# Column maxima of the pooling logits through DRAM, W_out's squares summed over all blocks before one norm product, and a new order

## The chip, the cores and the metric

The kernel runs on one core of one Trainium2 chip. The core has five engines that run side by side, each through its own list of instructions in order: TensorE (PE in the profile, with its weight loads as PEld), VectorE (DVE), ScalarE (ACT), GpSimd (POOL) and SyncE (SP), which here issues nearly all DMA transfers. An instruction waits on semaphores for what it needs from other engines or from a transfer, and everything behind it on its engine waits too. The metric is the device time of one execution in microseconds, the median over runs; lower is better.

## The reference, cut to what matters

```python
a = exp(phi - max(phi, over the 576 positions)); a = a / (sum(a) + 1e-9)
k_m = einsum('bhsm,bhsd->bhmd', a, k)       # 8 batches, 8 heads, 576 positions,
v_m = einsum('bhsm,bhsd->bhmd', a, v)       # 64 dims, pooled to 32 memory rows
scores = q @ k_m.T / 8
attn = exp(scores - max(scores)); attn = attn / (sum(attn) + 1e-9)
x = attn @ v_m                              # 4608 tokens x 512
h = x @ w_in                                # 512 x 2048
g = h - tanh(h)
out = g @ w_out                             # 2048 x 512
```

The weights arrive as 64-bit floats and are converted on the chip. Every float is carried as a sum of two fp16 parts, high and low (`hi`, `lo` for weights, `ah`, `al` for the attention, `ph`, `pl` for v_m times w_in), and a product is three fp16 matmuls. For `g` a short polynomial in h is used that holds for small h. A check of the sizes of the data decides at the end whether that was allowed; if not, a slow path (`wide_path`) recomputes everything. For that check the kernel sums the squares of W_in's and W_out's columns.

## The kernel before, in words

The order of the work is one table, `ORDER`: each word is a step with its indices, and the kernel records the steps in that order. `in_order` then ties every instruction to the one before it on its engine, so the table fixes each engine's list. A step with several parts (a Python generator) appears as often as it has parts: `H0.0 ... H0.0` is the matmuls first and the square later. An `x` behind a word chooses the other PSUM buffer.

The words that matter here:

- `i6:kv3`, `o2:gg`, `k1:q`: a load of a weight block of W_in, of W_out, or of a block for the check, into the buffer named behind the colon. `T` converts a pair of blocks (lines 447, 450, 453 on VectorE, then 464 on ScalarE), and `L`, `Lv`, `Lp` make the low part on GpSimd, VectorE or TensorE.
- `FX`, `FQ`, `FA`: loads of the pooling logits of a batch, once as rows (`pt`, for the maximum) and once turned (`e`, for the products). `KA`, `KB`, `KR`, `Q`, `QT`: loads of k and v, and of q; `QT` uses the buffer `qt`.
- `X`, `XP`, `Y` or `YM`, `YE`: the softmax of the logits (below). `V`: pooling on TensorE (line 271). `N`: its norm on VectorE. `U`, `UV`: the transposition and its high and low parts.
- `S`, `AM`, `AE`, `AD`, `AT`, `AS`: scores, softmax and its two fp16 halves (`ah`, line 562; `al`, line 564), in two halves of the positions. A `v` marks VectorE in place of GpSimd.
- `P`, `PL`: v_m times w_in and its low part. The tokens come in 18 units of 256 and the 2048 columns of W_in in four blocks: `H` (line 622, 24 matmuls of 256 columns) makes h for one unit and block, `a` or `ap` the cubic on VectorE and ScalarE (lines 642, 644, 646), `g`, `c`, `f`, `s` the fp16 parts, `M` (lines 750 and 769) the product with W_out, `E` and `O` the output.
- `CW`, `SI`, `SS`, `NI`, `SO`, `NO`: the check's window of the weights (lines 495 and 496 on ScalarE or 498 on VectorE) and the sums of squares of W_in and W_out. `Z`: matmuls on constants, which keep TensorE busy while the first data come.

In batches 0 and 1 the softmax of the logits runs on rows. In batches 2 to 7, `X` (`top`) takes each row's maximum over the positions (line 191), giving a value per partition for two halves, and multiplies the identity by it (line 193, `dg`, in the buffer `qt`). `XP` (`top_all`) multiplies ones by `dg` on TensorE (line 202, fp32), so that every partition holds all 256 maxima in PSUM (`pmx`). `Y` subtracts them from `e` on VectorE, straight from PSUM (lines 210 and 213, batches 2 and 3). `YM` has ScalarE copy them to SBUF (line 221, `ms`) and GpSimd subtract (batches 4 to 7). `YE` is the exponential.

For W_out's norms, `SO` squares a quarter of the matrix (line 521), `SS` adds its four blocks of 128 rows to one (line 508), and `NO` multiplies by ones, four matmuls for four blocks of columns (line 529), with a copy to `wn` (line 531). Four quarters make 16 matmuls, and VectorE adds the four results (line 535).

Of the kernel before, what the change touches and what calls it, by code (L numbers as in the profile page):

```python
# [71 lines left out]
Z0.0 i0:gg i1:gg T0 T0 T0 T0 Z0.0 Z0.0 Z0.0 Z0.0 Z0.0 i6:kv3 T3 T3 T3 Z0.0 Z0.0 Z0.0 Z0.0 Z0.0 FX0 T3 Z0.0 Z0.0 Z0.0 Z0.0 Z0.0 X0 Lp0 Lp0 YX0 Z0.0  # L72
Z0.0 Lp3 Lp3 Z0.0 XT0 i2:gg i3:pp5 T1 T1 T1 i4:kv2 T1 XT0 XU0x T2 KA0 XU0 Z0.0 T2 T2 V0.0 Z0.0 Z0.0 Lv1 KB0 V0.1 N0 T2 L2 L2 U0x UV0 o2:gg Z0.0 Z0.0
o3:gg Z0.0 T9 T9 T9 U0 Q0.0 S0.0x S0.0 Q0.1 S0.1 UV0 KA1 P0.0x P0.0 P0.1 PLp0.0 AM0.0 AM0.0 AE0.0 P0.1 PLp0.1 o4:gg o5:pp2 S0.1 AM0.1 AM0.1 AD0.0
AD0.0 AE0.1 AD0.1 W0 AT0.0 T10 T9 AD0.1 AT0.1 PLp0.1 AS0.0 Q1.0 AS0.0 PLp0.0 Lp9 H0.0x ASv0.1 T10 ASv0.1 H1.0 Lp9 T10 T10 L10 o6:gg o7:gg H1.1 H0.0
# [4 lines left out]
g2.0 M2.0 i12:kv2 T12 T12 T12 Y2 a2.1 CW1 H3.0 c2.0 T12 a2.1 Lv4 o11:gg T13 T13 P0.2 P0.2 M2.0 a2.1 H3.1 i14:kv3 g2.1 KA2 c2.1 ap3.0 FA3 PL0.2 YE2  # L80
Lv12 ap3.0 ap3.0 V2.0 V2.1 T6 P1.2x T13 M2.1 H3.1 M2.1 T6 T6 T13 g3.0 a3.1 N2 U2x P1.2 Lv13 PL1.2 a3.1 OP2 T6 OP2 UV2 T7 T7 T7 H0.2x H0.2 a3.1 g3.1 T7
Lv6 H1.2 H1.2 M3.0 c3.0 M3.0 a0.2 Lv7 ap1.2 a0.2 a0.2 P0.3 o12:kv2 T14 ap1.2 o14:kv3 Q2.1 BS0 U2 c3.1 g0.2 M3.1 M3.1 c0.2 P0.3 PL0.3 H1.3x ap1.2 T15
OP3 OP3 UV2 H0.3 T15 g1.2 H1.3 FQ3 c1.2 T15 H0.3 M0.2 T15 L15 a1.3 a1.3 S2.1 T14 T14 T14 S2.0x a0.3 a0.3 S2.1 S2.0 P1.3x P1.3 a1.3 g1.3 a0.3 P2.0 g0.3
AMv2.0 PL1.3 M0.2 L14 c1.3 c0.3 H2.2 H2.2 AMv2.0 AM2.1 AM2.1 a2.2 AE2.0 ADv2.0 P2.0 a2.2 H2.3 H2.3 a2.3 M1.2 M1.2 PL2.0 a2.2 BF0 g2.2 cv2.2 H3.2 L15
P2.1 H3.2 L14 M1.3 a2.3 a2.3 BH0 BL0 M1.3 ADv2.0 W2 AT2.0 ap3.2 P2.1 R1 O1 O1 AE2.1 ap3.2 ap3.2 PL2.1 BS1 BF1 AS2.0 AS2.0 M0.3 M0.3 H4.0 H4.0 ap4.0 R0
P2.2 H3.3 g2.3 c2.3 O0 O0 BH1 BL1 AD2.1 AD2.1 ap4.0 ap4.0 M2.2 R2 X3 g3.2 c3.2 P2.2 PL2.2 H3.3 H4.1 H4.1 ap3.3 ap3.3 g4.0 ap4.1 ap4.1 KR3.0 XP3 Y3
f4.0 s4.0 M2.2 QT3.0 ap3.3 g3.3 s4.0 YE3 cv4.0 M2.3 M2.3 H4.2 O2 O2 c3.3 ap4.1 AT2.1 R3 H4.2 BS2 P2.3 AS2.1 P2.3 g4.1 AS2.1 V3.0x PL2.3 ap4.2 ap4.2
BF2 BH2 M3.2 f4.1 ap4.2 f4.2 M3.2 H4.3x s4.1 KR3.1 s4.1 BL2 V3.1 N3 k4:q XX M3.3 M3.3 H4.3 ap4.3 ap4.3 g4.2 U3x U3 UV3 M4.0 M4.0 cv4.1 UV3 S3.0x ap4.3
O3 O3 P3.0 M4.0 M4.0 S3.0 AMv3.0 P3.0 M4.1 H5.0 BS3 AMv3.0 AE3.0 f4.3 k0:e g4.3 cv4.3 M4.1 M4.1 M4.1 PL3.0 c4.2 s4.2 s4.2 P3.1 H5.0 a5.0 a5.0 M4.2
sv4.3 H5.1 CW4 BF3 a5.0 BH3 BL3 H5.1 g5.0 k2:q c5.0 M4.2 M4.2 f5.0 QT3.1 M4.2 H5.2 s5.0 sv4.3 M4.3 P3.1 a5.1 ADv3.0 a5.1 M4.3 M4.3 PL3.1 S3.1 ADv3.0  # L90
s5.0 a5.1 AT3.0 M4.3 H5.2 S3.1 E4 g5.1 a5.2 a5.2 E4 CW2 f5.1 E4 E4 sv5.1 P3.2 M4.3 H5.3 H5.3 FQ4 M5.0 FA4 M5.0 a5.2 cv5.1 E4 E4 AS3.0 a5.3 sv5.1 M5.0
M5.0 CW0 AS3.0 H6.0 M5.1 M5.1 M5.1 M5.1 f5.2 a5.3 g5.2 KR4.0 cv5.2 s5.2 s5.2 a5.3 H6.0 a6.0 f5.3 a6.0 a6.0 P3.2 H6.1 s5.3 H6.1 f6.0 M5.2 M5.2 M5.2
M5.2 P3.3 g5.3 c5.3 s5.3 M5.3 ap6.1 ap6.1 PL3.2 H6.2 ap6.1 g6.1 P3.3 AM3.1 AM3.1 c6.1 AE3.1 X4 XP4 g6.0 M5.3 c6.0 s6.0 PL3.3 f6.1 H6.2 a6.2 KR4.1 M5.3
Ev5 Ev5 M5.3 s6.0 Ev5 Ev5 Ev5 a6.2 ADv3.1 ADv3.1 YM4 M5.3 s6.1 Ev5 a6.2 YM4 YE4 H6.3 H6.3 s6.1 QT4.0 AT3.1 ap6.3 ap6.3 M6.0 M6.0 AS3.1 AS3.1 g6.2 k3:e
f6.2 M6.0 sv6.2 V4.0 M6.1 M6.1 ap6.3 g6.3 f6.3 M6.0 M6.1 M6.1 sv6.3 sv6.2 H7.0 H7.0 a7.0 c6.2 V4.1 N4 W3 a7.0 sv6.3 M6.2 SI0 H7.1 a7.0 f7.0 H7.1 a7.1
U4 UV4 FQ5 UV4 M6.2 QT4.1 M6.2 a7.1 M6.2 U4 H7.2 H7.2 SSv0 NI0 a7.1 f7.1 a7.2 c6.3 M6.3 NI0 g7.0 a7.2 a7.2 s7.0 S4.0 c7.0 S4.0 AMv4.0 M6.3 M6.3 E6
s7.0 g7.2 c7.2 H7.3 H7.3 E6 a7.3 M6.3 E6 s7.1 E6 E6 W4 g7.1 M6.3 E6 s7.1 P4.0 P4.0 S4.1x S4.1 AMv4.1 a7.3 X5 CW3 AMv4.0 AE4.0 a7.3 g7.3 M7.0 M7.0 M7.0
M7.0 H8.0 H8.0 f7.2 c7.1 M7.1 M7.1 M7.1 M7.1 s7.2 f7.3 PL4.0 ap8.0 ap8.0 AMv4.1 AD4.0 ap8.0 XP5 s7.2 k5:e sv7.3 CW5 cv7.3 M7.2 KR5.0 AD4.0 f8.0 g8.0
M7.2 M7.2 M7.2 sv7.3 AE4.1 ADv4.1 s8.0 s8.0 c8.0 AT4.0 H8.1 YM5 ADv4.1 H8.1 P4.1 P4.1 M7.3 M7.3 a8.1 a8.1 a8.1 H8.2 AS4.0 PL4.1 M7.3 Ev7 H8.2 a8.2 FA5
QT5.0 YM5 a8.2 YE5 f8.1 M7.3 Ev7 P4.2 P4.2 g8.1 M7.3 AS4.0 c8.1 s8.1 s8.1 Ev7 Ev7 a8.2 g8.2 Ev7 H8.3 M8.0 Ev7 M8.0 c8.2 M8.0 V5.0 M8.1 AT4.1 AS4.1  # L100
KR5.1 PL4.2 H9.0 H8.3 a8.3 a8.3 a8.3 H9.0 f8.2 a9.0 a9.0 s8.2 s8.2 M8.1 M8.1 V5.1 f8.3 P4.3x P4.3 N5 s8.3 k6:e M8.0 M8.1 g8.3 H9.1x H9.1 a9.0 PL4.3
U5x s8.3 UV5 ap9.1 f9.0 M8.2 M8.2 UV5 ap9.1 ap9.1 c8.3 f9.1 M8.2 M8.2 M8.3 g9.0 c9.0 M8.3 SI1 k7:q SS1 U5 S5.0 g9.1 M8.3 sv9.0 k8:e E8 E8 H9.2 E8 E8
S5.0 M8.3 M8.3 AS4.1 H9.2 H9.3x sv9.0 CW6 ap9.2 ap9.2 ap9.2 QT5.1 c9.1 M9.0 M9.0 M9.0 E8 E8 s9.1 s9.1 AM5.0 H9.3 a9.3 AM5.0 f9.2 a9.3 FQ6 a9.3 NI1x
# [33 lines left out]
class Attention:  # L137


    def __init__(self, tc, c, big, place, ins):  # L140
# [47 lines left out]
    def top(self, b, d):  # L188
        nc, big = self.tc.nc, self.big
        mx = big.tile([P, 2], F32, tag="mx", name=f"mx{b}")  # L190
        nc.vector.tensor_reduce(mx, d["pt"], axis=AX.X, op=ALU.max)
# [1 line left out]
        nc.vector.tensor_tensor(
            dg, self.c["ident"].unsqueeze(1).to_broadcast((P, 2, P)),
            mx.unsqueeze(2).to_broadcast((P, 2, P)), op=ALU.mult,
# [945 lines left out]
```

## Time and profile before

| | |
|---|---|
| median of 3 runs | 635.82 us (635.75 to 637.44) |
| the profiled execution | 636.29 us |
| its span, first to last instruction | 634.2 us |
| granted TensorE clock, mean | 0.996 |
| TensorE busy | 619.4 us |
| VectorE busy | 570.9 us |
| ScalarE, GpSimd busy | 428.7, 350.5 us |
| moved by DMA | 85.03 MB |

In the profile, a group's row gives line, engine, operation, output from input by the names in the kernel, shape and count, then busy time in all and the mean of one in ns, then the idle time ahead of it and who ended it. A row of waits gives who waited for whom, the total in us, how often, and the longest. A row of the timeline gives start and duration in us. The rows by stretch give busy time and count of instructions for each engine, the granted clock (1 is full), the share of the DMA engines' time and GB/s. Durations of neighbouring matmuls overlap, so what one holds the array for is read from start to start.

### The profile page before, as it was taken

The numbers are of one execution on the slowest core, as the hardware profiler recorded it, in microseconds if no ns is written. First come the engines' busy times: TensorE is split into PE (matmuls) and PEld (weight loads), VectorE is DVE, ScalarE is ACT, GpSimd is POOL, SyncE is SP. The second block draws the span as 40 slices with busy tenths as digits, with TensorE's granted clock in tenths as the row PEclk, the third lists the DMA queues.
The fourth block names the chain that finished last, engine by engine and source line by source line (L and its number), as shares of the span: only waits on it lengthen the run. The fifth ranks groups of instructions, "written<-read, shape, count | busy, mean of one in ns | idle before, by whom it ended". The sixth has DMA issues, their size and how long they took to land.

```text
span 634.2 us, 16291 instructions
## 1 busy us (share of the span) xinstructions
PE 619.4 (98%) x6908; PEld 485.5 (77%) x6908; DVE 570.9 (90%) x763; ACT 428.7 (68%) x601; POOL 350.5 (55%) x314
## 2 busy tenths in 40 slices
...
GB/s 342 416 269 274 252 264 158 118 73 68 184 138 145 65 56 72 73 167 112 116 85 122 113 67 149 109 88 173 38 41 163 118 103 89 49 153 35 166 100 39
DMA packets 25872, 85.03 MB, mean 134 GB/s; under 512 B 2752, under 2 KB 2752, under 8 KB 25024
## 3 DMA queue, kind: packets, MB, share of 16 engines
...
## 4 chain that ended last, share of the span: by engine, by line
PE 86%; DVE 7%; DMA 4%; ACT 1%; issue 1%; SPq 0%; DVEq 0%; ACTq 0%
PE h L622 27%; PE x L769 22%; PE o L769 16%; PE o L750 10%; PE pp L573 3%; PE o1h L750 3%; DMA raw<-in_w_out_dram 3%; PE pkv L271 2%; DMA pt<-in_phx_dram 1%; PE psc L323 1%; DVE h L642 1%; DVE wt L450 1%; DVE wt L453 1%; DVE h L646 1%; DVE bw L709 0%
## 5 line engine op out<-in xcount | busy, mean ns | idle before, releaser
L622 PE MATMUL h<-ah,ph 128*128 128x256 f16 (+3 forms) x1536 | 201.0, 246 | 0.7 <-DVE h L642 0.7
L622 PEld LDWEIGHTS <-ph 128*128 128x128 f16 x2304 | 178.2, 98 | 20.7 <-issue 3.7
L672 POOL TENSOR_TENSOR g<-h,g 128x512 f16<-128x512 f32 x114 | 128.3, 1147 | 100.4 <-ACT g L666 94.2
L622 PE MATMUL h<-al,ph 128*128 128x256 f16 (+3 forms) x768 | 170.0, 246 | 1.1 <-POOL al L564 1.1
L693 POOL TENSOR_TENSOR f<-s,f 128x512 f16<-128x512 f32 x86 | 107.3, 1269 | 86.1 <-ACT f L689 81.1
L769 PEld LDWEIGHTS <-f 128*128 128x128 f16 x1344 | 129.1, 98 | 20.8 <-issue 5.2
L769 PE MATMUL x<-bt,f 128*128 128x256 f16 x1008 | 128.3, 273 | 0.0
L644 ACT ACTIVATE u<-u,beta 128x1024 f32<-128x1024 f32 x72 | 82.5, 1146 | 46.8 <-DVE h L642 46.5
L769 PEld LDWEIGHTS <-g 128*128 128x128 f16 x1008 | 97.9, 98 | 14.7 <-issue 3.5
L629 ACT ACTIVATE u<-h 128x1024 f32<-128x1024 f32 x72 | 73.3, 1018 | 47.6 <-PE h L622 31.4
L642 DVE SCALAR_TENSOR_TENSOR h<-h,u 128x1024 f32<-128x1024 f32 x72 | 87.9, 1221 | 19.2 <-ACT u L629 17.6
L646 DVE SCALAR_TENSOR_TENSOR h<-u,h 128x1024 f32<-128x1024 f32 x72 | 92.7, 1289 | 11.7 <-ACT u L644 11.4
L666 ACT ACTIVATE g<-h 128x512 f16<-128x512 f32 (+2 forms) x128 | 68.2, 579 | 19.9 <-DVE h L646 13.4
L750 PEld LDWEIGHTS <-g 128*128 128x128 f16 x384 | 36.7, 98 | 45.2 <-issue 3.0
L689 ACT ACTIVATE f<-s 128x1024 f16<-128x1024 f32 x56 | 58.6, 1048 | 11.1 <-DVE s L682 7.0
L750 PE MATMUL o<-wout_hi,g 128*128 128x512 f16 x192 | 59.0, 379 | 0.0
L680 DVE TENSOR_TENSOR s<-h 128x512 f32<-128x512 f32 x56 | 45.3, 808 | 2.0 <-DVE h L646 0.5
L769 PE MATMUL o<-wout_hi,f 128*128 128x256 f16 x224 | 45.9, 273 | 0.0
L769 PE MATMUL o<-wout_hi,g 128*128 128x256 f16 x224 | 45.8, 273 | 0.0
L769 PE MATMUL x<-wout_hi,g 128*128 128x256 f16 x224 | 45.8, 273 | 0.0
L769 PE MATMUL o<-bt,g 128*128 128x256 f16 x336 | 45.3, 273 | 0.0
L586 ACT ACTIVATE ph<-pp 128x1024 f16<-128x1024 f32 x32 | 32.4, 1014 | 18.4 <-PE pp L573 17.6
...
## 6 DMA issues: line engine op xcount, KB each, us to landing
...
chk<-in_w_in_dram SPq DMA_DIRECT2D x16, 512.0 KB, 4.1
chk<-in_w_out_dram SPq DMA_DIRECT2D x16, 512.0 KB, 3.8
out_dram<-r SPq DMA_DIRECT2D x27, 256.0 KB, 2.3
...
raw<-in_w_out_dram SPq DMA_DIRECT2D x12, 512.0 KB, 8.6
```

Of the source, the lines that this page charges most:

```text
L622: nc.tensor.matmul(hp[:, k, tu : tu + w], px[:, g, cs], d[ax][:, g, ta : ta + w], start=(n == 0), stop=(n == 5),)
L629: nc.scalar.activation(uu, hp, AF.Square, scale=1.0 / (S_A * S_P))
L642: nc.vector.scalar_tensor_tensor(t, hp, C2 * S_G / (S_A * S_P), uu, op0=ALU.mult, op1=ALU.mult)
L644: nc.scalar.activation(uu, uu, AF.Square, bias=c["beta"])
L646: nc.vector.scalar_tensor_tensor(h3, uu, CC, t, op0=ALU.add, op1=ALU.mult)
L666: nc.scalar.activation(hi, x, AF.Copy)
L672: eng.tensor_tensor(lo[:, ks], x[:, ks], hi[:, ks], op=ALU.subtract)
L680: nc.vector.tensor_tensor(s[:, 0:2], pair, a_block(h3, 0, 0).unsqueeze(1).to_broadcast((P, 2, 2, P)), op=ALU.add)
L689: nc.scalar.activation(f[:, 0], s, AF.Copy)
L693: eng.tensor_tensor(f[:, 1, ks], s[:, ks], f[:, 0, ks], op=ALU.subtract)
L750: nc.tensor.matmul(o, gx[:, k, P * tt : P * tt + P], wx[:, 4 * fb + k, :], start=(first and k == 0 and wx is wout_hi and gx is gh), stop=( ...
L769: nc.tensor.matmul(dst, a(na, kk), b(nb, kk), start=(new and kk == 0 and na == 0 and nb == 0), stop=(end and kk == 1 and na == 1))
```

## The change

`X` no longer builds `dg`. It writes the 256 maxima to a small DRAM tile, and `XP` reads them back into every partition of an SBUF tile `ms`; `Y` and `YM` both subtract from there. `SS` now also adds W_out's quarters to each other, in the fp16 tile `wn`, and `NO` stands once, with four matmuls. The bounds of W_out's window are a little narrower. The table `ORDER` is written anew throughout. Numbers of lines of the kernel after are some 10 lower.

```diff
-WO_WIN = (1.002 * 2.0 ** -6, 3.493)
+WO_WIN = (1.004 * 2.0 ** -6, 3.486)
...
 ORDER = """
-T11 T11 FX1 X1 o1:gg YX1 a0.0 o0:pp2 L10 H1.0 XT1 Z0.0 T11 T8 T8 T8 XT1 XU1 XU1 a1.0 a0.0 KB1 V1.0 a0.0 V1.1 T8 Lv8 a1.0 g0.0 H1.1 c0.0 N1 T11 L11
...
+o10:pp5 H0.0x H1.0 H0.0 a0.0 H1.0 a1.0 o0:pp2 H1.1 YX1 XT1 XT1 a0.0 H0.1 XU1 XU1 T11 V1.0 o1:gg T8 T8 T8 T8 KB1 V1.1 a0.0 o9:pp4 g0.0 Lv8 H1.1 i10:kv3
...
         mx = big.tile([P, 2], F32, tag="mx", name=f"mx{b}")
         nc.vector.tensor_reduce(mx, d["pt"], axis=AX.X, op=ALU.max)
-        dg = big.tile([P, 2, P], F32, tag="qt", name=f"dg{b}", bufs=1)
-        nc.vector.tensor_tensor(
-            dg, self.c["ident"].unsqueeze(1).to_broadcast((P, 2, P)),
-            mx.unsqueeze(2).to_broadcast((P, 2, P)), op=ALU.mult,
-        )
-        d["dg"] = dg
-
-    def top_all(self, b, d, early=False):
-        nc, dg = self.tc.nc, d["dg"]
-        pa = self.psum(f"pmx{b}", early)
-        nc.tensor.matmul(pa[:, 0, 0:256], self.c["ones"], dg.rearrange("p a b -> p (a b)"), start=True, stop=True)
-        d["px"] = pa
+        d["md"] = self.dram.tile([2, P], F32, tag=f"md{b}", name=f"md{b}")
+        nc.sync.dma_start(d["md"].rearrange("r p -> p r"), mx)
+
+    def top_all(self, b, d):
+        d["ms"] = m = self.big.tile([P, 256], F32, tag="ms", name=f"ms{b}", bufs=1)
+        row = d["md"].rearrange("r p -> (r p)").unsqueeze(0).to_broadcast((P, 256))
+        self.tc.nc.sync.dma_start(m, row)
...
-    def expo(self, b, d):
-        self.less_top(self.tc.nc.vector, d["e"], d["px"][:, 0, 0:256])
-
-    def expo_pool(self, b, d):
-
-        m = self.big.tile([P, 256], F32, tag="qt", name=f"ms{b}", bufs=1)
-        self.tc.nc.scalar.activation(m, d["px"][:, 0, 0:256], AF.Copy)
-        yield
-        self.less_top(self.tc.nc.gpsimd, d["e"], m)
+    def expo(self, b, d, eng=None):
+        self.less_top(eng or self.tc.nc.vector, d["e"], d["ms"])
...
         sq = acc["q", i]
-        for k, m in ((0, 2), (1, 3), (0, 1)) if eng is nc.gpsimd else ((slice(0, 2), slice(2, 4)), (0, 1)):
+        steps = [(0, 2), (1, 3)] if eng is nc.gpsimd else [(slice(0, 2), slice(2, 4))]
+        for k, m in steps:
             eng.tensor_tensor(sq[:, k], sq[:, k], sq[:, m], op=ALU.add)
+        if ("n", i) in acc:
+            if i == 0:
+                acc["n"] = big.tile([P, 512], F16, tag="wn", name="wn", bufs=1)
+            to = acc["n"] if i == 0 else sq[:, 0]
+            eng.tensor_tensor(to, sq[:, 0], sq[:, 1], op=ALU.add)
+            if i > 0:
+                eng.tensor_tensor(acc["n"], acc["n"], sq[:, 0], op=ALU.add)
+        else:
+            eng.tensor_tensor(sq[:, 0], sq[:, 0], sq[:, 1], op=ALU.add)
...
     def norms_out(part):
-        if part == 0:
-            acc["n"] = big.tile([P, 4, 4], F32, tag="wn", name="wn", bufs=1)
-        sq = acc.pop(("q", part))
         pa = place(f"pno{part}")
         for k in range(4):
-            nc.tensor.matmul(pa[:, 0, k : k + 1], sq[:, 0, P * k : P * k + P], c["ones16"], start=True, stop=True)
-        yield
-        nc.scalar.activation(acc["n"][:, :, part], pa[:, 0, 0:4], AF.Copy, scale=(S_W * S_Q) ** -2)
-        yield
-        if part == 3:
-            o = N_CHECK - 4
-            nc.vector.tensor_reduce(stat[:, o : o + 4], acc["n"], axis=AX.X, op=ALU.add)
+            nc.tensor.matmul(pa[:, 0, k : k + 1], acc["n"][:, P * k : P * k + P], c["ones16"], start=True, stop=True)
+        yield
+        nc.scalar.activation(stat[:, N_CHECK - 4 : N_CHECK], pa[:, 0, 0:4], AF.Copy, scale=(S_W * S_Q) ** -2)
...
-        "Y": lambda b: att.expo(b, st[b]), "YM": lambda b: att.expo_pool(b, st[b]), "YE": lambda b: att.expo_exp(b, st[b]),
+        "Y": lambda b: att.expo(b, st[b]), "YM": lambda b: att.expo(b, st[b], nc.gpsimd), "YE": lambda b: att.expo_exp(b, st[b]),
```

Counted over the whole list of each engine, the new order also moves some work between engines: on VectorE the window reductions go from 13 to 18 (on ScalarE from 19 to 14), the subtractions of the scores' maxima from 6 to 2 (on GpSimd from 10 to 14), the divisions from 6 to 8, the low halves `al` from 2 to 4, and the low parts `f` and `g` by one block each. What the other engines' lists show of the change stands in the prediction, piece by piece.

More of the change, by code (lines that the diff above doesn't have):

```diff
@@ L71 @@
 ORDER = """
[L72 to L75, printed above, removed]
@@ L80 @@
[L80 to L83, printed above, removed]
@@ L84 @@
[L84 to L103, printed above, removed]
@@ L124 @@
-k24:q SSv2 NO2x M14.3 M14.3 AS7.1 CW23 k30:q f15.1 s15.1 Ev14 Ev14 Ev14 M14.3 s15.0 Ev14 M15.0 M15.0 a15.2 CWv13 NO2 AS7.1 H16.0 g15.1 s15.1 c15.1
-H15.3 a15.3 a15.3 g15.2 CW24 M15.0 M15.0 Ev14 Ev14 f15.2 s15.2 a15.3 cv15.2 M15.1 M15.1 H16.0 a16.0 SO3 M15.1 M15.1 CWv30 s15.2 M15.2 a16.0 f15.3
-sv15.3 SSv3 H16.1 a16.0 f16.0 H16.1 g15.3 c15.3 NO3 NO3 M15.2 M15.2 ap16.1 ap16.1 k14:q k16:q sv15.3 ap16.1 f16.1 s16.0 s16.0 H16.2x H16.2 ap16.2 CW14
-M15.3 g16.0 cv16.0 M15.3 M15.3 E15 g16.1 cv16.1 M15.2 M15.3 ap16.2 M15.3 E15 H16.3 CW16 k29:q ap16.2 f16.2 M16.0 M16.0 E15 E15 H17.0x H16.3 a16.3
```

101 lines of the change are left out of this document (67 added, 34 removed).

## The prediction

> **What bounds the kernel now.** I read the page first: the busy times and the shares of the chain.
>
> ```profile
> span 634.2 us, 16291 instructions
> PE 619.4 (98%) x6908; PEld 485.5 (77%) x6908; DVE 570.9 (90%) x763; ACT 428.7 (68%) x601; POOL 350.5 (55%) x314
> ...
> PE 86%; DVE 7%; DMA 4%; ACT 1%; issue 1%; SPq 0%; DVEq 0%; ACTq 0%
> ```
>
> TensorE is busy for 98% of the span, and the chain that ended last runs through it for 86%. An average hides the stages, so next I asked for the busy time in five stretches, and for what TensorE waited for.
>
> ```profile
> core 0: us, PE busy (x) PEld busy (x) DVE busy (x) ACT busy (x) POOL busy (x), PEclk, DMA share, GB/s
> 0.00:54.00 54.00, 45.31 (x482) 26.36 (x483) 44.51 (x75) 32.58 (x44) 12.62 (x25) 0.97 0.89 352
> 54.00:100.00 46.00, 46.00 (x486) 26.11 (x484) 44.58 (x56) 33.26 (x44) 23.67 (x18) 1.00 0.62 222
> 100.00:200.00 100.00, 100.00 (x1014) 62.65 (x1012) 97.07 (x112) 64.51 (x76) 55.21 (x41) 1.00 0.34 119
> 200.00:620.00 420.00, 418.73 (x4862) 362.28 (x4847) 378.58 (x506) 296.97 (x437) 255.32 (x229) 1.00 0.31 103
> 620.00:634.20 14.20, 9.31 (x87) 8.12 (x84) 6.16 (x18) 1.36 (x3) 3.70 (x4) 0.95 0.12 44
> ```
>
> ```profile
> PE pkv L271 <- ACT e L259: 2.1, 2, 1.5
> ...
> PE ptr L311 <- DVE kvn L288: 1.1, 2, 0.9
> PE h L622 <- DVE h L642: 0.7, 1, 0.7
> PE pkv L255 <- ACT e L247: 0.7, 1, 0.7
> ```
>
> TensorE idles 54.00 - 45.31 = 8.69 us in the opening, which waits for loads (DMA share 0.89) and for the first two batches' attention. It idles nothing from 54 to 200, 1.27 us from 200 to 620, and 4.89 us in the tail. Between 54 and 620 us the time is TensorE's work, one for one. From 54 to 200 VectorE is nearly as full (141.65 of 146 us), so a wait on VectorE there has little slack before it reaches TensorE.
>
> **What the change takes from TensorE.** Here is one of the six column-maximum products in place, then one of the four groups of norm products, each with the next matmul behind it, and then where all of them lie.
>
> ```profile
> 448.78 0.60 PE L202 MATMUL pmx<-dg,ones 128*128 128x256 f32 x2
> 449.21 0.27 PE L769 MATMUL x<-bt,f 128*128 128x256 f16 x1
> ...
> 511.11 0.24 PE L529 MATMUL pno<-ones,sqo 128*128 128x1 f16 x4
> 511.21 0.27 PE L769 MATMUL x<-bt,f 128*128 128x256 f16 x1
> ...
> L202 PE MATMUL pmx<-dg,ones x12: 379/380/462, 83.2 to 449.0; 128*128 128x256 f32 x12
> ...
> L529 PE MATMUL pno<-ones,sqo x16: 163/163/177, 511.1 to 568.7; 128*128 128x1 f16 x16
> ```
>
> The durations overlap, so I take start to start. A maximum holds the array for 449.21 - 448.78 = 0.43 us (its two records are one fp32 matmul), a norm group for 0.10 us. Six maxima go, 6 x 0.43 = 2.58 us, and three of four norm groups, 3 x 0.10 = 0.30 us: 2.88 us. All lie between 83 and 569 us, where TensorE idles at most 1.27 us, so 2.88 us comes off the span unless something else is late there. No other count on TensorE differs: warm-ups, P, H and M blocks are as many as before.
>
> **What moves on VectorE.** The rows, with the new count from the order behind them:
>
> ```profile
> L193 DVE TENSOR_TENSOR dg<-ident,mx 128x256 f32<-128x256 f32 x6 | 3.4, 570 | 0.2
> ...
> L498 DVE TENSOR_REDUCE stat<-chk 128x1 f32<-128x512 f32 x13 | 8.7, 672 | 0.0
> L353 DVE TENSOR_TENSOR sc<-sc,sm 128x576 f32<-128x576 f32 x6 | 6.0, 1007 | 0.0
> L368 DVE TENSOR_TENSOR sc<-sc,sz 128x576 f32<-128x576 f32 x6 | 5.6, 937 | 0.0
> L564 DVE TENSOR_TENSOR al<-af,ah 128x576 f16<-128x576 f32 x2 | 1.6, 795 | 0.0
> L693 DVE TENSOR_TENSOR f<-s,f 128x1024 f16<-128x1024 f32 x13 | 17.9, 1379 | 0.0
> L672 DVE TENSOR_TENSOR g<-h,g 128x512 f16<-128x512 f32 (+2 forms) x28 | 20.0, 753 | 0.0
> L508 DVE TENSOR_TENSOR sqo<-sqo 128x1024 f16<-128x1024 f16 (+1 forms) x6 | 3.3, 554 | 0.1
> ```
>
> Six dg go (-3.42 us) and four subtractions of the softmax maximum (-4.03). Added are five window reductions (+3.36), two divisions (+1.87), two al (+1.59), one f (+1.38), two g (+1.51), four instructions of squares (+2.22), and four additions into wn at up to 0.55 us (+2.2). The net is +6.7 us, 570.9 to 577.6, still 91% of the span. Up to batch 3's norm, which is about the stretch from 54 to 200, the lists differ by two dg, one g pair and one subtraction less, and one window reduction and one division more: -1.14 - 1.51 - 1.01 + 0.67 + 0.94 = -2.0 us. So the added work lies behind 200 us, where VectorE has 420 - 378.58 = 41 us free, and costs nothing while that cover lasts; without it, up to 6.7 us. ScalarE and GpSimd, with 200 us and more free, shed work: the ms and wn copies, five window squares, GpSimd's squares.
>
> Batches 2 and 3 subtract the maximum from SBUF now, not PSUM; the nearest row is VectorE's 1.22 us below (85.02), and I take the same. The Trainium skill, GPSIMD Engine Reference, section Specifications, says that GpSimd shares its SBUF interfaces with VectorE and that instructions with two SBUF inputs contend. No run here shows that for this one. [...]
>
> **The trip through DRAM.** In the engine that issues the loads (SyncE), around batch 2's maxima, md2 and ms2 being the new write and read and raws12, raw27 weight blocks, the rows before are
>
> ```order
> L152 DMA pt2_1089<-in_phx_dram 128x1152
> L430 DMA raw24_1100<-in_w_out_dram 128x512
> L436 DMA raws12_1159<-in_w_in_dram 128x2x512
> L430 DMA raw27_1182<-in_w_out_dram 128x512
> L436 DMA raws14_1250<-in_w_in_dram 128x2x512
> ```
>
> and in the same place now
>
> ```order
> L152 DMA pt2_967<-in_phx_dram 128x1152
> L193 DMA md2_971<-mx2_969 128x2x1
> L424 DMA raws12_1034<-in_w_in_dram 128x2x512
> L418 DMA raw27_1105<-in_w_out_dram 128x512
> L198 DMA ms2_1193<-md2_971 128x256
> L161 DMA kv20_1265<-in_kva_dram 128x2064
> ```
>
> SyncE issues in order: md2 waits for VectorE's maximum, and raws12, raw27 and the loads behind wait with it; ms2 waits until md2 has landed, and kv20 and raws14 wait for that. The trace of before has no such small write; its nearest rows are the two halves of the partial outputs' trip, then the W_out loads, and VectorE around batch 2:
>
> ```profile
> raw<-in_w_out_dram SPq DMA_DIRECT2D x12, 512.0 KB, 8.6
> ...
> d<-ot ACTq DMA_DIRECT2D x8, 256.0 KB, 3.7
> ...
> pr<-d SPq DMA_DIRECT2D x8, 256.0 KB, 3.3
> ...
> DMA to landing us min/median/max: 2.0/3.7/7.3
> ...
> DMA to landing us min/median/max: 2.0/2.6/5.6
> ...
> 81.94 0.76 DVE L447 TENSOR_SCALAR wt<-raw 128x512 uint32<-128x512 uint32 x2
> ...
> 83.82 1.28 DVE L453 SCALAR_TENSOR_TENSOR wt<-raw,wt 128x512 uint32<-128x512 uint32 x2
> 85.02 1.22 DVE L210 TENSOR_TENSOR e<-e,pmx 128x1024 f32<-128x1024 f32 x1
> ...
> 86.76 1.23 DVE L642 SCALAR_TENSOR_TENSOR h<-h,u 128x1024 f32<-128x1024 f32 x1
> ```
>
> Write and read together: 3.7 + 3.3 = 7.0 us, from 4.0 to 7.3 + 5.6 = 12.9 us. Between batch 2's maximum and its subtraction VectorE's new list holds four steps of cubics (4 x 1.23 us), two short pairs of weight conversions (2 x 0.76) and four long ones (4 x 1.28), and a g of 1024 (two means of L672, 1.5): 13.1 us. So the trip is hidden at 7.0 us, with little to spare at its worst. raw27 is used 9.9 us behind the maximum (the same list up to its first step). It is issued about 2 us behind it, after raws12, whose buffer the first conversion frees; at the row's 8.6 us it lands at 10.6, 0.7 us late. I take zero for both and keep 1 + 0.7 us. For batch 3, ms3 is issued behind the two stores of unit 0's outputs, with six VectorE instructions of some 6.8 us ahead of its use, against 0.7 + 3.3 us: zero. From batch 4 on GpSimd subtracts, which is free 45% of the time, and it does so 9 to 124 words of the order behind the read: zero.
>
> The Trainium skill, DMA: Bandwidth & Descriptors, section Rules for kernel authors, speaks against this write: where the last dimension is not contiguous, it becomes one descriptor per element, here 256 of four bytes. [...]
>
> **The new order in the opening.** On VectorE, in the second half of batch 0's attention: al0 is what the second unit's first block (H1.0, written h10) needs, wt10 a weight block. Before:
>
> ```order
> L450 SCALAR_TENSOR_TENSOR wt10_469<-raw20_445,wt10_469 128x512
> L450 SCALAR_TENSOR_TENSOR wt10_469<-raw21_447,wt10_469 128x512
> L564 TENSOR_TENSOR al0_477<-af0_467,ah0_476 128x2x288
> L453 SCALAR_TENSOR_TENSOR wt10_469<-raw20_445,wt10_469 128x512
> L453 SCALAR_TENSOR_TENSOR wt10_469<-raw21_447,wt10_469 128x512
> ```
>
> Now:
>
> ```order
> L438 SCALAR_TENSOR_TENSOR wt10_449<-raw20_370,wt10_449 128x512
> L438 SCALAR_TENSOR_TENSOR wt10_449<-raw21_447,wt10_449 128x512
> L441 SCALAR_TENSOR_TENSOR wt10_449<-raw20_370,wt10_449 128x512
> L441 SCALAR_TENSOR_TENSOR wt10_449<-raw21_447,wt10_449 128x512
> L555 TENSOR_TENSOR al0_489<-af0_444,ah0_488 128x2x288
> ```
>
> ```profile
> 37.51 0.27 PE L622 MATMUL h<-al,ph 128*128 128x256 f16 x1 [1.11 <-POOL al L564]
> ...
> 38.53 0.75 DVE L564 TENSOR_TENSOR al<-af,ah 128x576 f16<-128x576 f32 x1
> 39.20 1.28 DVE L453 SCALAR_TENSOR_TENSOR wt<-raw,wt 128x512 uint32<-128x512 uint32 x2
> ...
> 46.13 0.59 PE L858 MATMUL warm<-nid 128*128 128x512 f16 x2
> ```
>
> al0 moved behind both third steps, from 39.28 to 39.20 + 1.28 = 40.48 us. H0.0 runs 24 matmuls of 0.109 us from 37.51 to 40.13 us, and H1.0 needs al0 from its second, at 40.24: a new wait of 0.24 us. On TensorE, batch 1's transposes pet stood together with pkv before H0.1 (the second block of unit 0); now H0.1 stands between them. That hides the 0.7 us that pkv's transposes waited for ScalarE and drops the warm-up pair there, 0.59 us; but nothing covers the norm in front of ptr any more, which cost batch 0 0.9 us and batch 1 only 0.2: +0.7. Together 0.24 - 1.29 + 0.7 = -0.35 us. I count zero, since the first M block also waits for VectorE's cubic and weights, whose list up to there is longer by one low half of a weight; the ends are -1.1 and +0.9. The tail stands word for word as before.
>
> **The sum.** The profiled execution took 636.29 us, 2.09 around its span of 634.2. 634.2 - 2.88 = 631.3, with 2.09 around it 633.4. The median of the runs is 635.82, so 632.9 us. A measurement of this kernel tells about 0.3%, 1.9 us: faster is below 633.9, slower above 637.7.
>
> **The rivals.** *More than the products*: the opening comes out at its good end (-1.1) and the 1.27 us idle between 200 and 620 goes, since dg and ms leave their buffer. 635.82 - 2.88 - 1.1 - 1.27 = 630.6 us. For it: the q loads' buffer (qt) is free earlier. Against it: nothing in the trace ties that idle time to a q load. 0.08. *The gain is eaten*: the opening at +0.9, raw27 0.7 and ms2 1 us late while VectorE and TensorE are both full: -2.88 + 2.6 = -0.3, 635.5 us. For it speaks that 4.35 us is all that VectorE has free from 54 to 200; against it, that it is 2.0 us lighter there now. 0.24. *The write to DRAM is long* (slower): SyncE stands at ms2 until md2 is done, VectorE stands at the subtraction behind it, and kv20 and the weights behind are late with it. Below 13.1 us for the trip it costs nothing; it makes the kernel slower from 13.1 + 2.88 + 1.9 = 17.9 us on, and at 20 us it adds 6.9: 635.82 - 2.88 + 6.9 = 639.8 us. For it: four-byte elements, of which the trace has none. Against it: 256 KB take 3.7 us, and this is 1 KB. 0.10. By the page's one descriptor per element, 256 of them would have to take 0.06 us each in turn for this. That the products do not go is no rival, since the new order has no pmx row.
>
> **How the numbers follow.** The forecast has 0.58. Its own range, with the opening's ends, is 631.8 to 633.8. Faster: 0.58 + 0.08 = 0.66, less a little for ends that meet: 0.65. Same: 0.24, with that, 0.25. Slower: 0.10. The range runs from the first rival's 630.6 to 636.8, which holds the second with another 1.3 us, and leaves out the slow one.
>
> **What would show it.** TensorE busy about 616.5 us and idle near 14.9, with 46 of 46 us busy from 54 to 100: right. VectorE waiting for a DMA at ms, or at the weights behind md2, or more than 3 us of TensorE idle between 54 and 620: the write or the order is the cause, and the forecast is wrong. Idle time of TensorE up to its first o matmul that is over 1 us from 8.69 would mean that the opening's term was mis-sized. If the time falls and TensorE's busy time does not, the reason was another.

## The result, and the profile after

The changed kernel takes 645.94 us (median of six runs, 642.17 to 647.08) beside 635.85 us for the kernel before on the same chip (635.70 to 637.44): a ratio of 1.0146, 95% interval 1.0125 to 1.0166. It is 10.1 us slower; the forecast was 2.9 us faster. The profiled execution took 645.02 us.

Of the changed kernel's page, the span, the engines and the chain:

```profile
span 643.1 us, 16221 instructions
...
PE 618.2 (96%) x6884; PEld 483.9 (75%) x6884; DVE 567.1 (88%) x771; ACT 423.1 (66%) x579; POOL 335.4 (52%) x304
...
PE 64%; DVE 18%; DMA 5%; ACT 5%; issue 3%; POOL 2%; SPq 0%; DVEq 0%; ACTq 0%; POOLq 0%
```

TensorE's busy time fell only from 619.4 to 618.2 us, and its share of the chain from 86 to 64%; VectorE's rose from 7 to 18%, ScalarE's from 1 to 5%. The same five stretches as before:

```profile
0.00:54.00 54.00, 44.83 (x483) 25.84 (x484) 46.05 (x76) 31.31 (x42) 11.05 (x24) 1.00 0.93 352
54.00:100.00 46.00, 40.73 (x368) 22.50 (x366) 39.38 (x48) 28.63 (x35) 26.48 (x17) 1.00 0.73 216
100.00:200.00 100.00, 98.97 (x1043) 62.12 (x1044) 96.31 (x110) 68.05 (x79) 51.09 (x39) 0.98 0.35 125
200.00:620.00 420.00, 415.46 (x4826) 357.35 (x4825) 371.61 (x512) 287.07 (x413) 237.00 (x217) 1.00 0.33 101
620.00:643.10 23.10, 18.25 (x168) 16.13 (x166) 13.79 (x28) 8.03 (x14) 9.75 (x10) 1.00 0.28 95
```

TensorE's idle time per stretch (length less busy) is now 9.17, 5.27, 1.03, 4.54 and 4.85 us, in place of 8.69, 0, 0, 1.27 and 4.89: 10.0 us more. More than half of the new idle time lies between 54 and 100 us, where TensorE never stopped before. The longest of TensorE's waits (us in total, times, longest):

```profile
PE pkv L259 <- DVE ph L582: 4.2, 1, 4.2
```

This is batch 2's pooling, which waits for VectorE. So I followed batch 2 back. First SyncE's issues there, then VectorE (start, duration, and in brackets the idle time before it and what ended it), then a piece of the chain, which is the W_out block's load, from issue to landing:

```profile
77.00 0.38 SPq L193 DMA_DIRECT2D md<-mx  x1
78.81 0.38 SPq L424 DMA_DIRECT2D raws<-in_w_in_dram  x1
79.28 0.42 SPq L418 DMA_DIRECT2D raw<-in_w_out_dram  x1
86.17 0.34 SPq L198 DMA_DIRECT2D ms<-md  x1
```

```profile
87.79 1.23 DVE L637 SCALAR_TENSOR_TENSOR h<-u,h 128x1024 f32<-128x1024 f32 x1 [2.13 <-ACT u L635]
...
93.11 0.43 DVE L435 TENSOR_SCALAR wt<-raw 128x512 uint32<-128x512 uint32 x1 [3.75 <-DMA raw<-in_w_out_dram]
...
97.71 1.21 DVE L205 TENSOR_TENSOR e<-e,ms 128x1024 f32<-128x1024 f32 x1
...
99.46 1.23 DVE L582 SCALAR_TENSOR_TENSOR ph<-pp,ph 128x1024 f16<-128x1024 f32 x1
```

```profile
79.28 13.80 DMA raw<-in_w_out_dram
```

The write of batch 2's maxima, 1 KB, is issued at 77.00 us and releases SyncE at 86.17: 9.2 us. But VectorE doesn't stand at the subtraction. It stands 3.75 us at the weight block raw27, which was issued at 79.28 and landed 13.80 us later. Behind that come g and two steps of the conversion, which take 1.65 and 1.64 us beside GpSimd's part of g (0.68 us each at 80.7), and the subtraction follows them without a wait. VectorE also stands 2.13 us for ScalarE, which is itself held up:

```profile
86.23 0.33 ACTq L826 DMA_DIRECT2D d<-ot  x1
86.61 1.15 ACT L635 ACTIVATE u<-u,beta 128x1024 f32<-128x1024 f32 x1 [2.93 <-DMA md<-mx]
```

ScalarE could issue its own store, d<-ot, only at 86.23 us; the profile puts that wait down to md's landing. What the DMA engines moved from 80 to 88 us, by the view of the transfers, in the changed kernel:

```profile
DMA packets 59, 0.25 MB, mean 32 GB/s; under 512 B 0, under 2 KB 0, under 8 KB 58
```

and in the same 8 us of the kernel before:

```profile
DMA packets 836, 2.76 MB, mean 344 GB/s; under 512 B 63, under 2 KB 63, under 8 KB 817
```

The two weight blocks, 1.5 MB together, had been issued, yet almost nothing moved. In the trace's packet records, the pieces of four bytes all begin between 77 and 79 us, though the write lands only at 86.17. Behind them packets of 4 KB, 0.2 us in the median of the kernel before, take up to 7.7 us there; 32 of them take over 1.2 us between 80.0 and 88.8 us. The same shows, weaker, behind the writes of batch 4 (23 packets over 1.2 us, up to 4.6, at 209 to 217 us) and batch 5 (17, up to 3.9, at 307 to 318 us). Before, no packet takes over 2 us. The rows of the issues (times, KB, median us to landing, as far as the trace has the landings) show it for whole transfers; before, the first two stood at 8.8 and 8.6 us:

```profile
raws<-in_w_in_dram SPq DMA_DIRECT2D x6, 1024.0 KB, 11.5
raw<-in_w_out_dram SPq DMA_DIRECT2D x12, 512.0 KB, 9.8
...
ms<-md SPq DMA_DIRECT2D x6, 128.0 KB, 5.9
...
md<-mx SPq DMA_DIRECT2D x6, 1.0 KB, 7.8
```

Last, TensorE's granted clock (the third number from the right) directly behind the stop:

```profile
100.00:104.00 4.00, 3.22 (x64) 0.57 0.01 4
```

This low stretch costs up to 4 x 0.43 = 1.7 us of full work. The kernel before has one such stretch too, at 28 to 32 us, so how much of it is a net loss the two profiles don't say.

**The theories.** A: the 256 pieces of four bytes hold up the other transfers, and the loads behind them make VectorE and TensorE wait. B: the trip's own length costs, with SyncE standing between its two halves. C: the new order costs, whatever way the maxima take.

### The profile page after: what moved, and what is told of

The parts are those of the page before. It is cut to its first block, busy times and chain, and to the rows that moved or that the text cites. A ratio compares the mean times of both kernels' runs of the same rounds, so it can differ in the third digit from the quotient of the medians.

```text
span 643.1 us, 16221 instructions
## 1 busy us (share of the span) xinstructions
PE 618.2 (96%) x6884; PEld 483.9 (75%) x6884; DVE 567.1 (88%) x771; ACT 423.1 (66%) x579; POOL 335.4 (52%) x304
## 2 busy tenths in 40 slices
DMA packets 28368, 85.82 MB, mean 133 GB/s; under 512 B 4480, under 2 KB 5248, under 8 KB 27520
## 4 chain that ended last, share of the span: by engine, by line
PE 64%; DVE 18%; DMA 5%; ACT 5%; issue 3%; POOL 2%; SPq 0%; DVEq 0%; ACTq 0%; POOLq 0%
PE h L613 20%; PE x L760 18%; PE o L760 14%; PE o L741 5%; DVE h L637 2%; DVE h L633 2%; PE pp L564 2%; DMA raw<-in_w_out_dram 2%; PE pkv L259 2%; DMA pt<-in_phx_dram 2%; PE o1h L741 2%; DMA chk<-in_w_in_dram 2%; DVE wt L438 1%; DVE wt L441 1%; ACT u L635 1%
## 5 line engine op out<-in xcount | busy, mean ns | idle before, releaser
L663 POOL TENSOR_TENSOR g<-h,g 128x512 f16<-128x512 f32 x112 | 120.6, 1100 | 138.2 <-ACT g L657 125.8
L684 POOL TENSOR_TENSOR f<-s,f 128x512 f16<-128x512 f32 x84 | 104.4, 1264 | 79.5 <-ACT f L680 74.8
L680 ACT ACTIVATE f<-s 128x1024 f16<-128x1024 f32 x56 | 58.7, 1049 | 18.2 <-DVE s L673 12.9
L671 DVE TENSOR_TENSOR s<-h 128x512 f32<-128x512 f32 x56 | 41.2, 736 | 1.9 <-POOL f L684 0.3
L577 ACT ACTIVATE ph<-pp 128x1024 f16<-128x1024 f32 x32 | 32.3, 1013 | 11.2 <-PE pp L564 10.1
```

Source lines behind the costliest of these rows:

```text
L663: eng.tensor_tensor(lo[:, ks], x[:, ks], hi[:, ks], op=ALU.subtract)
L671: nc.vector.tensor_tensor(s[:, 0:2], pair, a_block(h3, 0, 0).unsqueeze(1).to_broadcast((P, 2, 2, P)), op=ALU.add)
L680: nc.scalar.activation(f[:, 0], s, AF.Copy)
L684: eng.tensor_tensor(f[:, 1, ks], s[:, ks], f[:, 0, ks], op=ALU.subtract)
```

## The experiments

Ratios are to the kernel before on the same chip, with the 95% interval. The plainest trial of C, the new order with all six maxima back on TensorE, has no time: with its words moved by a few places that order deadlocks.

**Batch 2 alone back on TensorE.** For batch 2 the diagonal and the product are put back, one word of the order moves:

```
+        if b == 2:    # in top: the diagonal as before the change, not shown
...
+        if b == 2:    # in top_all
+            pa = self.psum(f"pmx{b}")
+            self.tc.nc.tensor.matmul(pa[:, 0, 0:256], self.c["ones"], d["dg"].rearrange("p a b -> p (a b)"), start=True, stop=True)
+            d["ms"] = pa[:, 0, 0:256]
-  c2.1 XP2 Y2 YE2 PL0.2 H3.1
+  c2.1 PL0.2 XP2 Y2 YE2 H3.1
```

> As the changed kernel, but batch 2 alone goes back to the diagonal and the TensorE product; batches 3 to 7 still go through DRAM. If the write of batch 2 is what costs most: idle in 80 to 100 us under 1 us, and 645.9 - 5.3 (idle at 80 to 100) - 1.0 (the clock's low stretch behind it) = 639.6 us, 638 to 641. If the order is the cause: over 644 us.

Measured: 650.82 us, 1.0216 (1.0174 to 1.0258); five runs lie between 645.16 and 652.95 us. A sixth, left out of the ratio, took 2265.62 us at full granted clock; why is not known. TensorE and the W_out block in the trace, of the run of 645.60 us:

```profile
PE pmx L205 <- DVE ph L597: 4.7, 1, 4.7
...
DMA to landing us min/median/max: 4.6/5.9/7.1
```

It doesn't tell A from C by its time, since my edit made a wait of its own: the product needs the PSUM tile that the P block in front of it still holds, and TensorE stood 4.7 us for it. What it does show is that without the write batch 2's W_out block lands 7.1 us behind its issue (13.80 with it), with no slow packet at 78 to 90 us.

**The maxima in rows of 128 bytes.** VectorE transposes 32x32 blocks, so that 32 maxima lie side by side in a partition:

```
-        mx = big.tile([P, 2], F32, tag="mx", name=f"mx{b}")
-        nc.vector.tensor_reduce(mx, d["pt"], axis=AX.X, op=ALU.max)
+        mx = big.tile([P, 2, 32], F32, tag="mx", name=f"mx{b}")
+        nc.vector.memset(mx[:, 0], 0.0)
+        nc.vector.tensor_reduce(mx[:, 0, 0:2], d["pt"], axis=AX.X, op=ALU.max)
+        nc.vector.transpose(mx[:, 1], mx[:, 0])
-        nc.sync.dma_start(d["md"].rearrange("r p -> p r"), mx)
+        for r in range(2):
+            rows = mx[:, 1].rearrange("(q s) j -> s q j", s=32)[r]
+            nc.sync.dma_start(d["md"][r].rearrange("(q j) -> q j", j=32), rows)
```

> As the changed kernel, but VectorE transposes the maxima in 32x32 blocks first, and they are written as eight pieces of 128 bytes in two transfers in place of 256 pieces of 4 bytes. If the pieces of 4 bytes are what holds the DMA engines up: the write lands in 2 to 4 us in place of 7.8, no read packet behind it takes over 2 us, the W_out block lands 10 us behind its issue in place of 13.8, and the time falls to 637 to 641 us. If it is the trip itself, two transfers one behind the other with SyncE standing between them: the write still takes over 6 us or TensorE still idles over 3 us at 80 to 100 us, and the time stays over 643 us.

Measured: 634.68 us, 0.9982 (0.9971 to 0.9993). That is 11.3 us below the changed kernel, 1.0 below the 635.65 us of the kernel before, and below both of my ranges. Two of its stretches, SyncE and VectorE at batch 2:

```profile
54.00:100.00 46.00, 46.00 (x485) 25.99 (x484) 45.17 (x59) 33.94 (x39) 25.66 (x18) 1.00 0.58 214
...
200.00:620.00 420.00, 417.85 (x4839) 361.69 (x4838) 378.30 (x525) 291.78 (x417) 235.58 (x215) 1.00 0.31 103
```

```profile
77.01 1.18 SPq L197 DMA_DIRECT2D md<-mx  x2
78.41 0.38 SPq L428 DMA_DIRECT2D raws<-in_w_in_dram  x1
78.84 1.53 SPq L422 DMA_DIRECT2D raw<-in_w_out_dram  x1
80.47 0.37 SPq L202 DMA_DIRECT2D ms<-md  x1
```

```profile
88.21 1.28 DVE L442 SCALAR_TENSOR_TENSOR wt<-raw,wt 128x512 uint32<-128x512 uint32 x2
89.42 1.22 DVE L209 TENSOR_TENSOR e<-e,ms 128x1024 f32<-128x1024 f32 x1
```

The read is issued 3.5 us behind the write, VectorE waits for nothing, the subtraction starts 8.3 us earlier than in the changed kernel, and TensorE is busy 46 of 46 us. The order, the trip and the new norms are all still there. So C falls as the cause of the loss, and A or B holds.

**Batch 2 alone scattered**, all others in rows:

```
+        if b == 2:
+            nc.sync.dma_start(d["md"].rearrange("r p -> p r"), mx[:, 0, 0:2])
+            return
```

> As the kernel with rows of 128 bytes (634.68 us), but batch 2's maxima are again written as 256 pieces of 4 bytes; batches 3 to 7 stay in rows. If batch 2's write is the place where the loss arises: read packets of over 2 us at 78 to 90 us alone, TensorE idle of 4 to 6 us at 80 to 100 us, and 634.7 + 5.3 + 1 to 2 (the clock) = 640 to 642 us. If the loss is spread over the six writes: 11.3 / 6 = 1.9 more, 636 to 637.5 us.

Measured: 641.91 us, 1.0097 (1.0081 to 1.0112). VectorE's wait, and the stretch:

```profile
DVE wt L442 <- DMA raw<-in_w_out_dram: 5.9, 1, 5.9
```

```profile
80.00:100.00 20.00, 16.57 (x147) 9.55 (x149) 13.96 (x20) 11.90 (x13) 4.41 (x3) 0.91 0.78 227
```

34 read packets of up to 7.9 us at 80 to 89 us, and none over 2 us elsewhere. By the ratios, batch 2 alone accounts for 0.0097 + 0.0018 = 0.0115, 7.3 us; the other five for 0.0146 - 0.0097 = 0.0049, 3.1 us. Which waits those 3.1 us are was not followed.

**Rows, and an unread scattered write behind them.** This takes SyncE's stand between write and read away and leaves the pieces:

```
+        if b == 2:
+            mu = self.dram.tile([2, P], F32, tag="mu", name="mu")
+            nc.sync.dma_start(mu.rearrange("r p -> p r"), mx[:, 0, 0:2])
```

> As the kernel with rows of 128 bytes (634.68 us), with one more write at batch 2 directly behind the rows: the same maxima as 256 pieces of 4 bytes into a tile that nobody reads. The trip that VectorE waits for stays short. If the pieces hold up the other transfers: W_out's blocks land 13 us behind their issue, VectorE stands 3 to 6 us for them, and the time is near the 641.91 us of the kernel in which batch 2's own write was scattered, 639.5 to 642.5. If the length of the trip itself was what cost: 634.5 to 636 us.

Measured: 642.64 us, 1.0110 (1.0095 to 1.0126). VectorE's one wait for a transfer at batch 2, SyncE's issue of the read, and the transfers from 80 to 88 us:

```profile
DVE wt L442 <- DMA raw<-in_w_out_dram: 6.5, 1, 6.5
```

```profile
80.67 0.37 SPq L205 DMA_DIRECT2D ms<-md  x1
```

```profile
DMA packets 78, 0.25 MB, mean 31 GB/s; under 512 B 17, under 2 KB 17, under 8 KB 78
```

SyncE issues the read of the maxima at 80.67 us, 3.2 us behind the first of the rows, and the loads behind it at once. The kernel is as slow as with batch 2's own write scattered, though nobody needs the pieces and SyncE doesn't stand for them. A holds at batch 2, and B's stand of SyncE is not needed for the loss. The trip doesn't stay short, as I had expected it to: the last of the read's 128 packets of 1 KB ends at 93.9 us, in the kernel with rows alone at 87.8. The read is held up like the weight block, which VectorE waits for until 93.8; what each of the two would cost alone was not separated.

**Unread writes in the kernel before.** The six scattered writes are added to the old order; the maxima still go through TensorE:

```
...
         d["dg"] = dg
+        md = self.dram.tile([2, P], F32, tag=f"md{b}", name=f"md{b}")
+        nc.sync.dma_start(md.rearrange("r p -> p r"), mx)
```

> The kernel before, with the six scattered writes of the maxima to DRAM added in its old order; nobody reads them, nobody waits for them, and the maxima still go through TensorE. If the scattered write holds up the other transfers: read packets of 2 to 7 us behind each write, loads that land 3 to 5 us later, and 636.5 to 641 us, as far as a load was just in time. If only the wait for the trip costs: 635.6 to 636.4 us, as before, and no long packets.

Measured: 656.94 us, 1.0314 (1.0292 to 1.0335), far above both of my ranges. Its writes and SyncE at batch 2, and VectorE's wait:

```profile
md<-mx SPq DMA_DIRECT2D x6, 1.0 KB, 9.3
```

```profile
79.56 0.38 SPq L199 DMA_DIRECT2D md<-mx  x1
80.04 0.42 SPq L432 DMA_DIRECT2D raw<-in_w_out_dram  x1
```

```profile
DVE wt L449 <- DMA raw<-in_w_out_dram: 10.9, 1, 10.9
```

Two costs are mixed: slow read packets (39 at 81 to 90 us, up to 7.2 us), and SyncE, which stands at md until VectorE has the maximum, so that the W_out block behind it is issued at 80.04 us in place of 71.74.

**The same unread writes, with the pieces apart.** Three kernels, with the piece or its place changed:

```
+        md = self.dram.tile([P, 2], F32, ...)           # 128 pieces of 8 bytes, side by side
+        nc.sync.dma_start(md, mx)

+        md = self.dram.tile([2, P, 128], F32, ...)      # 256 pieces of 4 bytes, 512 bytes apart
+        nc.sync.dma_start(md[:, :, 0].rearrange("r p -> p r"), mx)

+        md = self.dram.tile([2, P, 16], F32, ...)       # 256 pieces of 4 bytes, 64 bytes apart
+        nc.sync.dma_start(md[:, :, 0].rearrange("r p -> p r"), mx)
```

> The kernel before with six unread writes as before, but as 128 pieces of 8 bytes (a partition's two maxima together) in place of 256 of 4. If the cost goes by the number of pieces: landing 4 to 6 us, read packets up to 4 us, and 635.7 + 21.3 / 2 = 646 us, 641 to 650. If it goes by what lies under some size of piece: still 652 to 658 us. If 8 bytes are no longer harmful: 635.5 to 637 us.

> The kernel before with six unread writes of 256 pieces of 4 bytes, but each piece 512 bytes from the next in DRAM, so that no two touch the same 512 bytes. If the pieces hold each other up because they fall into the same 1 KB of DRAM: landing 2 to 4 us, no long read packets, 635.5 to 638 us. If the number and size of the pieces alone count: as the packed write, landing 8 to 11 us and 652 to 658 us.

> The kernel before with six unread writes of 256 pieces of 4 bytes, each piece 64 bytes from the next in DRAM (512 bytes apart: 1.7 us to landing and 642.28 us; packed: 9.3 us and 656.94). If pieces hold each other up only inside the same 64 bytes: landing about 1.7 to 2.5 us and 641.5 to 643 us. If inside a larger block of DRAM: landing 5 to 10 us, read packets of over 3 us, 646 to 657 us.

Measured: 642.47 us (1.0098, 1.0083 to 1.0113), 642.28 us (1.0102, 1.0087 to 1.0118) and 643.03 us (1.0115, 1.0100 to 1.0131). Their rows of the issues, in that order:

```profile
md<-mx SPq DMA_DIRECT2D x6, 1.0 KB, 3.9
```

```profile
md<-mx SPq DMA_DIRECT2D x6, 1.0 KB, 1.7
```

```profile
md<-mx SPq DMA_DIRECT2D x6, 1.0 KB, 2.2
```

The same 256 pieces of four bytes land in 1.7 us when they lie 512 bytes apart, in 2.2 us at 64, and in 9.3 us side by side. Apart, one read packet at most is over 2 us in the whole trace (2.1); side by side in pieces of 8 bytes they still reach 3.4 to 4.2 us, though that kernel is no slower than the one with the pieces 512 bytes apart. So it is neither the number of pieces nor their size alone, but their lying within the same few bytes of DRAM. That packing of four-byte pieces costs 0.0314 - 0.0102 = 0.0212, 13.5 us here. The 6.4 us that remain with the pieces 512 bytes apart, where I had expected 638 us at most, I read as SyncE's standing at the write: there, too, the W_out block is issued at 80.51 us and VectorE waits 3.6 us for it. No run tried that cost alone.

**Rows in the old order.** The kernel before, its norms too, with the maxima through DRAM in rows, in outline:

```
     def top(self, b, d):            # word X of the old order
-        the diagonal dg
+        maximum, transpose and two writes as in the kernel with rows
     def top_all(self, b, d):        # word XP
-        the product pmx
+        self.tc.nc.sync.dma_start(m, row)
     def expo, expo_pool             # words Y and YM: subtract m
```

> The kernel before in its old order and with its old norms, with the maxima of batches 2 to 7 through DRAM in rows of 128 bytes and the six products, six diagonals and four copies gone. If the trip fits the old order too: before less 2.6 for six products, 633 to 635.5 us. If the trip needs the new order (the old one has the read of the maxima directly behind the write, in front of the weights on SyncE's queue): idle of 2 us or more at 54 to 110 us, 637 to 642 us.

Measured: 651.51 us, 1.0238 (1.0224 to 1.0252), above both of my ranges. SyncE and VectorE at batch 2:

```profile
81.35 1.18 SPq L197 DMA_DIRECT2D md<-mx  x2
83.83 0.33 SPq L202 DMA_DIRECT2D ms<-md  x1
84.26 0.38 SPq L427 DMA_DIRECT2D raw<-in_w_out_dram  x1
```

```profile
DVE wt L444 <- DMA raw<-in_w_out_dram: 7.8, 1, 7.8
```

Without one packet over 2 us the trip costs 15.7 us here. At batch 2 the trace shows why: the loads stand behind a write that waits for VectorE, and the W_out block is issued at 84.26 us in place of 71.74. The new order with the same rows takes 634.68 us, so it is no loss of the changed kernel but the condition for using DRAM.

**The write on ScalarE's queue:**

```
-        nc.sync.dma_start(d["md"].rearrange("r p -> p r"), mx)
+        nc.scalar.dma_start(d["md"].rearrange("r p -> p r"), mx)
```

> The changed kernel with one edit: the six scattered writes of the maxima are issued by ScalarE on its own DMA queue, the reads back stay on SyncE. If the pieces of 4 bytes hold up the DMA engines or DRAM whatever queue they come from: write still 7 us or more to landing, W_out's block at batch 2 still over 12 us behind its issue, 643 to 648 us. If it is the order within SyncE's own queue that lets the loads stand behind the pieces: loads unhindered, 635 to 639 us.

Measured: 653.08 us, 1.0268 (1.0251 to 1.0285), worse than from SyncE. Two of its waits from 70 to 110 us:

```profile
ACT ot L824 <- DMA d<-ot: 4.0, 1, 4.0
...
ACT ot L824 <- DVE mx L191: 3.2, 1, 3.2
```

35 read packets of up to 8.4 us at 80 to 89 us, on the other queue: the pieces hold up SyncE's loads from ScalarE's queue just as well. ScalarE now also stands for the maximum (3.2 us) and for its own store behind the pieces (4.0 us).

**Products doubled.** The kernel before with each column-maximum product issued twice:

> The kernel before, with each of the six TensorE products that spread the maxima issued twice into the same PSUM tile; nothing else changes. If the first term of the sum holds (a product's 0.43 us goes one for one into the time): 635.8 + 6 x 0.43 = 638.4 us, 637.8 to 639. If TensorE's work is partly covered by waits that would stand there anyway: 635.8 to 637.3 us, and the gain of the change was counted too high.

```
         nc.tensor.matmul(pa[:, 0, 0:256], self.c["ones"], dg.rearrange("p a b -> p (a b)"), start=True, stop=True)
+        nc.tensor.matmul(pa[:, 0, 0:256], self.c["ones"], dg.rearrange("p a b -> p (a b)"), start=True, stop=True)
```

Measured: 637.88 us, 1.0031 (1.0019 to 1.0043): 1.2 to 2.7 us for six products, 2.3 by the medians, so 0.38 us each beside the 0.43 of the prediction. The first term was nearly right.

**One transfer for both rows**, eight pieces of 128 bytes:

```
+        mx = big.tile([P, 2, 2, 32], F32, tag="mt", name=f"mx{b}", bufs=1)
...
+        nc.vector.tensor_reduce(mx[:, 0, :, 0], d["pt"], axis=AX.X, op=ALU.max)
...
+        rows = mx[:, 1].rearrange("(q s) r j -> s q r j", s=32)[0]
+        nc.sync.dma_start(d["md"].rearrange("r (q j) -> q r j", j=32), rows)
```

> As the kernel with rows of 128 bytes, but both rows in one transfer of eight pieces (the transpose is 128x64, so that one partition in 32 holds both rows' 32 maxima): one issue of 0.5 us on SyncE less per batch. If SyncE's time and the trip are off the path by now: 634.3 to 635.0 us, the same as the 634.68 of two transfers. If the trip still decides somewhere: up to 1 us less, 633.6.

Measured: 634.56 us, 0.9989 (0.9977 to 1.0001). No difference to the two transfers: with rows, SyncE's second issue decides nothing. The one read of its maxima whose landing the trace has took 7.4 us, and it did no harm. The two kernels with rows are the fastest of all; the first is below the kernel before by its interval, the second is not.

## Why the prediction was wrong

The sum took two terms at zero, the trip through DRAM and the lateness of raw27. Both rested on the same premise, that a write of 1 KB costs little and leaves the loads beside it alone, and the runs show that it does not.

- **The products (-2.88): nearly right.** Doubling them costs 2.3 us of the 2.58 counted.
- **"So the trip is hidden at 7.0 us": the first step that failed.** I took the write from the partial outputs' stores, 256 KB in long rows, as its nearest row, and argued in the slow rival that 1 KB can't take longer than 256 KB. At batch 2 the write took 9.2 us (7.8 in the median of the landings), and the last packet of the read, issued at 86.17, ended at 93.3: 16.3 us for the trip, above the 12.9 that I had called the worst and above the 13.1 us of cover. VectorE's work alone would have brought it to the subtraction at 76.98 + 13.1 = 90.1 us, so the read was 3.2 us late there. No wait shows it, because VectorE stood longer in front of it. My upper bound was no bound, because no row of the trace had small pieces side by side. The page of the Trainium skill that I cited (DMA: Bandwidth & Descriptors, Rules for kernel authors) spoke against this write, and the trace agrees on the count: packets under 512 bytes rose from 2752 to 4480, of which 6 x 256 = 1536 are md's. I weighed that rule only as a longer trip. By its count I said that 256 pieces would have to take 0.06 us each to make the kernel slower; at batch 2 they took 9.2 / 256 = 0.036 us each in the mean, and that was enough.
- **"At the row's 8.6 us it lands at 10.6, 0.7 us late": the step that decided.** This lateness of raw27, which the sum took at zero, was worked out as though the write left its neighbours alone. It landed 93.08 - 76.98 = 16.1 us behind the maximum, 6.2 us behind the 9.9 at which VectorE wants it. VectorE waiting there was one of the signs of being wrong that I had named. The unread write behind the rows shows that the pieces by themselves, with nobody waiting for them, make the whole loss of batch 2: 0.0110 + 0.0018 = 0.0128, 8.1 us, beside the 7.3 of batch 2's own scattered write.
- **The slow rival: right in its culprit, wrong in its mechanism and its size.** It named the write, SyncE's stand at ms2 and the late weights. But it priced only the subtraction's wait: nothing below a trip of 13.1 us, and what lies above it one for one. At batch 2's 16.3 us that gives 635.82 - 2.88 + 3.2 = 636.1 us. The kernel took 645.94.
- **The order.** The opening's new wait of al0 was 0.24 us as forecast, the transposes in front of ptr wait 0.96 us longer (0.7 forecast), and one wait was not foreseen, of a P block (v_m times w_in) for vl, the low part of v_m, 1.33 us; together idle time rose by 0.48 us to 54 us, inside the term's ends:

```profile
30.25 0.41 PE L564 MATMUL pp<-win_hi,vh 64*32 64x512 f16 x8 [1.33 <-DVE vl L538]
...
40.42 0.27 PE L613 MATMUL h<-al,ph 128*128 128x256 f16 x1 [0.24 <-DVE al L555]
...
53.56 0.41 PE L299 MATMUL ptr<-ident,kvn 128*128 128x128 f32 x2 [1.14 <-DVE kvn L276]
```

- **VectorE's +6.7 us: wrong in size, without effect that shows.** Its busy time fell by 3.8. The three sums that make up each step `s` (lines 680 to 682 before), 168 of them before and after, shrank from 106.7 to 97.2 us. Of these, 114 ran before with GpSimd idle, at 0.50 us each, and 54 beside one of its instructions, for a part of their time at least, at 0.91; after the change it is 132 at 0.50 and 36 at 0.85. The fewer that run beside GpSimd account for the difference, though no run tried that alone. The two subtractions from SBUF took 1.21 us (1.22 taken), but GpSimd was idle beside both, so they don't try the contention that the Trainium skill, GPSIMD Engine Reference, section Specifications, speaks of. The 168 sums, which read both inputs from SBUF, agree with it.
- **What the mechanism is worth.** With the write made harmless, the same change gives 1.1 us by the ratio (0.4 to 1.8 by its interval) of the 2.9 forecast. In that kernel's profile TensorE's idle time is 2.0 us above before's: +0.39 to 54 us, +0.27 to 200, +0.88 to 620 and +0.45 in the tail. Which moves of the new order cause these was not separated.
